# The first modulation's scale as two TensorE rows in place of eight columns

## The chip, the core and the metric

The kernel runs on one core of a Trainium2 chip. The metric is the device time in microseconds (us) of one execution. The engines are named as the profile names them: PE (TensorE, with its weight loads as PEld), DVE (VectorE), ACT (ScalarE), POOL (GpSimd) and SP (SyncE, which issues the DMAs).

## What is computed

A transformer block of 2048 tokens with 1024 channels, all in fp32. A vector `c` of 1024 numbers modulates it: six vectors of 1024 come out of one product with `w_mod` (1024 x 6144), two of which, the shift `sa` and the scale `ca`, are needed before anything else.

```python
mod = (_silu(c) @ w_mod).reshape(c.shape[0], 6, 1, -1)
sa, ca, ga, sb, cb, gb = (mod[:, 0], mod[:, 1], mod[:, 2], mod[:, 3], mod[:, 4], mod[:, 5])
h = _layernorm(x, axis=-1) * (1 + ca) + sa
x = x + ga * _A_ref(h, A_wq, A_wk, A_wv, A_wo, A_beta)   # attention, 32 heads, 4 segments of 512 tokens
h = _layernorm(x, axis=-1) * (1 + cb) + sb
x = x + gb * _B_ref(h, B_w1, B_b1, B_w2, B_b2)           # MLP across the tokens
return x
```

The attention goes through four segments of 512 tokens; each segment's queries see their own segment by softmax and the earlier ones through a memory matrix.

## The kernel before

**The whole.** Products that must be nearly exact are made of three reduced products (`float32r`): each operand is split into a high part (a cast, L123 on ACT or L125 on DVE) and a low part (the difference, L126 on DVE or POOL). The order of the instructions on each engine comes from the tile framework's scheduler at build time, so it is fixed when the kernel runs: each engine takes its queue in order and waits on semaphores. The change lies in the first part, up to the projection of the first segment; the rest of the program (attention L322 to L650, the mixer from L814) is untouched.

**The first part, in the order of the code.**

- `sc` (L110) is silu of `c`, laid out as 128 partitions x 8; `scb` (L257 to L263) is the same vector as a row that stands on all 128 partitions, made by eight transposes into the banks `scps` and two copies.
- `load_x` (L210) fetches four x tiles of 128 tokens, x0 to x3, for segment 0; `norm_x` (L215) normalizes each: statistics on DVE (L131 to L139), the affine step on ACT (L218).
- The modulation loop (L278) goes over eight chunks `ct` of 128 channels. For each it fetches two tiles of `w_mod`, 512 KB each, in buffers `wm` (11 of them): part 0 for the shift, part 1 for the scale. The shift is one DVE instruction that multiplies the tile by `scb` and sums each row into `saca[:, ct, 0]` (L283). The scale is made in two ways: for the first four chunks (`NSC = 4`) by eight PE products with a 128x128 piece of the tile as the stationary operand and one column of `sc` moving (L291); for the last four by two POOL products with `scb` (L287) and a sum on ACT (L288). L295 adds 1 and puts it in `saca[:, ct, 1]`.
- Within the loop the first three rounds also fetch and split the projection's first weights (`load_part`, L164: `wv`, `wq`).
- `h_chunk` (L220) transposes one chunk of channels of the four x tiles (L223, into a bank `hps`), applies scale and shift on ACT while it reads the bank (L225), and splits the result: the cast on ACT, the difference on POOL in segment 0; in segment 1 the cast on DVE, the difference on POOL for even chunks and on DVE for odd ones.
- `first_chunk` (L267) adds one chunk to the projections of segment 0: 12 products for keys and values (L196, banks `nps`) and 3 for queries (L204, bank `qps`).

**What comes next.** `project(0, ...)` (L338) copies `nps` out on ACT (L358, L359, L364), transposes the keys (L373, bank `kps`), splits queries and keys into `sg` and makes phi of the keys (L391 and L392 on ACT, L394 on DVE). `seg_load(1)` (L560) fetches x4 to x7, behind the last modulation tile, and normalizes them; `seg_chunks(1, 0, 8)` makes segment 1's eight h chunks; `project(1, ...)` uses them. SP issues all these DMAs from one queue, in its program order; a DMA also waits for the eighth one before it.

## Time and profile before

| what | value |
|---|---|
| runs | 2251.84, 2254.03, 2257.36 us; median 2254.03 |
| profiled execution | 2248.92 us, of which the span is 2247.2 us |
| granted clock, mean | 0.998 |
| PE / DVE / ACT / POOL busy | 98% / 74% / 51% / 33% of the span |
| DMA | 423.06 MB, mean 188 GB/s |

How to read it. The page gives busy times over the span. A line of a timeline is: start in us from the span's start, duration in us (from the first start to the last end, where several like instructions are merged), engine, line of the code, operation, output tile <- input tiles, shape, count, and in brackets the idle time of the engine ahead of it and what ended it. Matmuls are pipelined: a record lasts longer than the distance to the next start, so a merged row holds one such tail. A plain fp32 matmul is recorded as two instructions, a `float32r` one and a transpose as one. A line of the windows gives, for one stretch, the busy time and count of PE, PEld, DVE, ACT and POOL, the granted clock, the DMA engines' busy share, and GB/s.

### The profile page before, as it was taken

What the parts mean: (1) busy time and instruction counts of PE and PEld (TensorE: products, weight loads), DVE (VectorE), ACT (ScalarE), POOL (GpSimd) and SP (SyncE); (2) the same over time, 40 slices, a digit from 0 to 9 for tenths busy, and PEclk for the clock granted to TensorE, in tenths of its full rate; (3) what the DMA queues carried; (4) which work ended last, traced back from release to release, by engine and by line L of the source; (5) the groups of instructions that cost most, each with busy time, mean ns of one, the idle gap of its engine ahead of it and who ended that gap; (6) DMA issues with size and microseconds to landing.
All of it is one profiled execution on the core that took longest, in us unless ns stands there. A gap on an engine that the chain in (4) does not pass through costs nothing.

```text
span 2247.2 us, 38365 instructions
## 1 busy us (share of the span) xinstructions
PE 2195.4 (98%) x13802; PEld 1892.9 (84%) x13802; DVE 1671.5 (74%) x3778; ACT 1145.6 (51%) x2106; POOL 748.6 (33%) x847
## 2 busy tenths in 40 slices
PE   7999999999999999999999999999999999999999
PEld 6879888888988888988888888888888888888887
DVE  6676777766767777655758866788888887868687
ACT  6476867765666656655546633533334242424232
POOL 5166657656666667654001200033330000000000
PEclk9999999999999999999999999999999999999999
DMA  6656565687666566664764587755556541414134
GB/s 263 204 169 174 160 185 161 199 283 239 176 182 207 168 188 193 190 198 164 229 220 151 215 333 262 262 190 221 206 202 238 203 154 57 155 57 146 57 122 150
DMA packets 175186, 423.06 MB, mean 188 GB/s; under 512 B 17524, under 2 KB 71828, under 8 KB 166036
## 3 DMA queue, kind: packets, MB, share of 16 engines
q1 hardware_dynamic: 174996, 420.61, 57.1%
q8 instruction: 110, 1.80, 0.3%
q14 instruction: 80, 0.66, 0.1%
HBM read 244.62 MB, written 125.06 MB: 165 GB/s over the span
## 4 chain that ended last, share of the span: by engine, by line
PE 83%; DVE 7%; DMA 3%; POOL 2%; ACT 2%; issue 2%; SPq 1%; ACTq 0%; DVEq 0%; POOLq 0%
PE mx L863 44%; PE nps L196 11%; PE po L733 8%; PE qps L204 7%; PE pv L505 3%; PE a L476 1%; PE sx L441 1%; PE sz L441 1%; POOL ph L491 1%; DMA wr<-in_w_dram 1%; DVE ac L870 1%; PE a L479 1%; PE rd L413 1%; PE a L483 1%; PE sy L441 1%
## 5 line engine op out<-in xcount | busy, mean ns | idle before, releaser
L863 PE MATMUL mx<-bU,sp 128*128 128x512 f32 x2352 | 534.7, 389 | 1.1 <-DVE ac L870 0.9
L863 PEld LDWEIGHTS mx<-bU,sp 128*128 128x128 f32 x2352 | 441.0, 188 | 94.3 <-issue 1.3
L196 PE MATMUL nps<-wv,h 128*128 128x256 f32 x3072 | 441.7, 284 | 4.7 <-POOL h L126 3.8
L123 ACT CAST sp<-wr 128x384 fp32r<-128x384 f32 (+2 forms) x408 | 217.1, 545 | 430.5 <-PE mx L863 349.6
L491 POOL TENSOR_TENSOR ph<-p,ph 128x640 f16<-128x640 f32 x256 | 378.5, 1499 | 170.2 <-ACT ph L489 169.6
L863 PE MATMUL mx<-bA,sp 128*128 128x512 f32 x1764 | 430.5, 389 | 0.0
L196 PEld LDWEIGHTS nps<-wv,h 128*128 128x128 f32 x3072 | 405.6, 190 | 13.1 <-POOL h L126 5.0
L863 PEld LDWEIGHTS mx<-bA,sp 128*128 128x128 f32 x1764 | 331.1, 188 | 68.8
L126 DVE TENSOR_TENSOR sp<-wr,sp 128x384 fp32r<-128x384 f32 (+2 forms) x408 | 260.1, 648 | 31.5 <-ACT sp L123 31.3
L870 DVE TENSOR_TENSOR ac<-mx,ac 128x512 f32<-128x512 f32 x280 | 189.9, 686 | 85.2 <-PE mx L863 84.8
L204 PE MATMUL qps<-h,wq 128*128 128x512 f32 x768 | 196.3, 397 | 0.0
L489 ACT CAST ph<-p 128x1280 f16<-128x1280 f32 x128 | 160.9, 1257 | 51.6 <-POOL p L487 50.9
L733 PE MATMUL po<-wo,ots 128*128 128x512 f32 x768 | 181.3, 391 | 0.0
L487 POOL TENSOR_SCALAR_AFFINE_SELECT p<-p 128x256 f32<-128x256 f32 x256 | 131.7, 524 | 108.4 <-ACT p L484 54.8
L733 PEld LDWEIGHTS po<-wo,ots 128*128 128x128 f32 x768 | 142.7, 188 | 29.1
L863 PE MATMUL mx<-bB,sp 128*128 128x512 f32 x588 | 164.0, 389 | 0.0
L204 PEld LDWEIGHTS qps<-h,wq 128*128 128x128 f32 x768 | 140.9, 189 | 26.8 <-ACT vp L364 0.3
L442 DVE CUSTOM_DVE_ANT_0 sx<-sx,mask 128x128 f32<-128x128 f32 (+1 forms) x256 | 110.6, 432 | 65.4 <-PE sx L441 63.6
L505 PE MATMUL pv<-vp,ph 128*128 128x97 bf16 (+1 forms) x2560 | 141.9, 202 | 5.2 <-DVE red L512 2.8
L505 PEld LDWEIGHTS <-ph 128*128 128x128 f16 x2560 | 113.6, 98 | 28.7 <-issue 11.9
L863 PEld LDWEIGHTS mx<-bB,sp 128*128 128x128 f32 x588 | 110.4, 188 | 22.9
L870 DVE TENSOR_TENSOR cc<-mx,cc 128x512 f32<-128x512 f32 x140 | 95.0, 685 | 38.3 <-PE mx L863 38.1
(200 smaller groups left out, 3191.7 us busy)
## 6 DMA issues: line engine op xcount, KB each, us to landing
sk<-sg SPq DMA_DIRECT2D x384, 128.0 KB
wr<-in_w_dram SPq DMA_DIRECT2D x28, 1024.0 KB
wr<-in_w_dram SPq DMA_DIRECT2D x32, 768.0 KB
bstu<-ucd SPq DMA_DIRECT2D x28, 768.0 KB
wsp<-wv SPq DMA_DIRECT2D x32, 512.0 KB
rawm<-in_wm_b_dram SPq DMA_DIRECT2D x32, 512.0 KB
wv<-wsp SPq DMA_DIRECT2D x32, 512.0 KB
pcd<-cc SPq DMA_DIRECT2D x14, 1024.0 KB
```

Of the source, the lines that this page charges most:

```text
L123: last_hi[0] = A.copy(hi, src)
L126: lo_eng.tensor_tensor(lo, src, hi.bitcast(F32), op=ALU.subtract)
L196: T.matmul(ps[:, aa], h[:, j, 128 * tt:128 * tt + 128], wt[:, i, o:o + 256], start=(n == 0), stop=(n >= 6 * NK - 2), skip_group_check=True)
L204: T.matmul(ps, wt[:, i, o:o + 128], h[:, j], start=(k + n == 0), stop=(3 * k + n == 3 * NK - 1))
L442: marks[4 * t + h - LEADS, "V"] = V.tensor_tensor_reduce(o, o, mask[:, 384 - 128 * i:], 1.0, -3.0e38, op0=ALU.add, op1=ALU.max, accum_out= ...
L487: G.affine_select(w, w, pattern=[[0, 2], [1, 128]], compare_op=ALU.is_ge, fill=0.0, base=0, channel_multiplier=-1)
L489: marks[n, "A"] = A.copy(ph[:, 0], p32)
L491: marks[n, "G"] = G.tensor_tensor(ph[:, 1, c], p32[:, c], ph[:, 0, c], op=ALU.subtract)
L505: T.matmul(pv[:, i, 0:w], ph[:, part, o:o + 128], d["vp"][:, j, h, 0:w], start=(n == 0), stop=(n == 19), skip_group_check=True)
L733: T.matmul(ps, os_[:, i, P * ct:P * ct + P], wop[ct, nh][:, j], start=(n == 0), stop=(n == 3 * NK - 1))
L863: T.matmul(ps, ops[q][:, i, P * k:P * k + P], b[:, j], start=(m == 0 and first), stop=(m == 3 * nk - 1), skip_group_check=True)
L870: V.tensor_tensor(d, ps, d, op=ALU.add)
```

## The change

The scale is no longer made chunk by chunk. The host lays its half of `w_mod` out anew, as eight tiles of 512 KB: tile `i` holds, for one half of the output channels (512 columns), two blocks of 128 inputs. PE makes each half as one row of 512: the stationary operand is one column of `sc` (128x1), the moving one the 128x512 block of `w_mod`, eight such plain fp32 matmuls add up in one bank (`srow`). DVE copies the row from PSUM into partition 0 of `bc`, PE turns each 128 of it into a column by a product with the 1x1 corner of the identity (four products a half, into the bank `scale`), and one DVE instruction a half adds 1 and writes four columns of `saca`. The POOL products, the ACT sums and `scs` are gone.

The eight scale tiles are fetched ahead: four before x0 to x3, four after them, all before the first shift tile. The shift is made as before.

```diff
@@ -253,6 +252,15 @@
+    scale_wm = []
+
+    def fetch_scale(i):
+        t = s1p.tile([P, 2, 512], F32, tag="wm", bufs=11, name=f"wms{i}")
+        SY.dma_start(t.rearrange("p a n -> p (a n)"), wm_a[1, i])
+        scale_wm.append(t)
+
+    for i in range(4):
+        fetch_scale(i)
     xs = {0: [load_x(s1p, tt) for tt in range(4)]}
@@ -273,26 +281,25 @@
     with tc.high_priority():
         for t in xs[0]:
             norm_x(s1p, t)
-    scale_ps = bank("ms", 1, "scale")
-    scs = s1p.tile([P, NK], F32, name="scs")
+    for i in range(4, 8):
+        fetch_scale(i)
+    scale_ps = bank("pv", 1, "scale")
+    rows = bc.rearrange("p a b -> p (a b)")[0:1]
+    for cb in range(2):
+        ps = bank(*(("ms", 1), ("s1", 2))[cb], f"srow{cb}")
+        for k in range(NK):
+            T.matmul(ps[0:1], sc[:, k:k + 1], scale_wm[4 * cb + k // 2][:, k % 2], start=(k == 0), stop=(k == NK - 1))
+        V.tensor_copy(rows[:, 512 * cb:512 * cb + 512], ps[0:1])
+        for ct in range(4 * cb, 4 * cb + 4):
+            T.matmul(scale_ps[:, ct:ct + 1], rows[:, P * ct:P * ct + P], ident[0:1, 0:1], start=True, stop=True,
+                     skip_group_check=True)
+        V.tensor_scalar_add(saca[:, 4 * cb:4 * cb + 4, 1], scale_ps[:, 4 * cb:4 * cb + 4], 1.0)
     for ct in range(NK):
-        for part in range(2):
-            wm = s1p.tile([P, D], F32, tag="wm", bufs=11, name=f"wm{ct}_{part}")
-            last_wm = SY.dma_start(wm, wm_a[part, ct])
-            if part == 0:
-                V.scalar_tensor_tensor(wm, wm, 1.0, scb, op0=ALU.mult, op1=ALU.mult, accum_out=saca[:, ct, 0:1])
-            elif ct >= NSC:
-                for i in range(2):
-                    c = slice(512 * i, 512 * i + 512)
-                    G.tensor_tensor(wm[:, c], wm[:, c], scb[:, c], op=ALU.mult)
-                A.activation(wm, wm, AF.Copy, accum_out=scs[:, ct:ct + 1])
-            else:
-                for k in range(NK):
-                    T.matmul(scale_ps[:, ct:ct + 1], wm[:, P * k:P * k + P], sc[:, k:k + 1], start=(k == 0),
-                             stop=(k == NK - 1), skip_group_check=True)
+        wm = s1p.tile([P, D], F32, tag="wm", bufs=11, name=f"wm{ct}")
+        last_wm = SY.dma_start(wm, wm_a[0, ct])
+        V.scalar_tensor_tensor(wm, wm, 1.0, scb, op0=ALU.mult, op1=ALU.mult, accum_out=saca[:, ct, 0:1])
         if ct < 3:
             load_part(0, 0, *(("v", 0), ("q", 0), ("v", 1))[ct], W[0, 0])
-        V.tensor_scalar_add(saca[:, ct, 1:2], (scale_ps if ct < NSC else scs)[:, ct:ct + 1], 1.0)
         h_chunk(s1p, xs[0], 0, ct)
         if ct:
             first_chunk(ct - 1)
@@ -1065,9 +1072,8 @@
-        "wm_a": np.stack([wm[:, :D].T.reshape(NK, P, D), np.concatenate([
-            wm[:, D:2 * D].reshape(NK, P, NK, P).transpose(2, 1, 0, 3).reshape(NK, P, D)[:NSC],
-            wm[:, D:2 * D].T.reshape(NK, P, D)[NSC:]])]),
+        "wm_a": np.stack([wm[:, :D].T.reshape(NK, P, D),
+                          wm[:, D:2 * D].reshape(4, 2, P, 2, 512).transpose(3, 0, 2, 1, 4).reshape(NK, P, D)]),
```

1 line of the change is left out of this document (removed).

## The prediction

> **What bounds the kernel now.** I read the page first, then busy time in windows of 10 us, then the timeline of the first 70 us, where the change lies.
>
> ```profile
> span 2247.2 us, 38365 instructions
> PE 2195.4 (98%) x13802; PEld 1892.9 (84%) x13802; DVE 1671.5 (74%) x3778; ACT 1145.6 (51%) x2106; POOL 748.6 (33%) x847
> ```
> ```profile
> 10.00:20.00 10.00, 7.81 (x36) 7.44 (x37) 8.40 (x30) 7.81 (x13) 0.00 (x0) 1.00 1.03 411
> ...
> 40.00:50.00 10.00, 7.20 (x51) 6.25 (x50) 6.66 (x25) 6.95 (x17) 9.01 (x8) 1.00 0.01 4
> 50.00:60.00 10.00, 7.55 (x48) 6.14 (x48) 4.96 (x12) 10.00 (x19) 5.68 (x14) 0.87 0.13 28
> 60.00:70.00 10.00, 9.38 (x76) 8.98 (x76) 9.16 (x13) 4.20 (x6) 4.46 (x5) 0.96 0.95 263
> 70.00:80.00 10.00, 9.98 (x68) 8.87 (x67) 4.22 (x11) 4.71 (x11) 0.00 (x0) 1.00 0.95 341
> ```
> PE is busy for 98% of the span, but not at its start. A window's columns are PE, PEld, DVE, ACT, POOL, granted clock, DMA share, GB/s. From 70 us on PE works 9.98 us of 10. Before that others lead: the transfers at 10 to 20 (share 1.03), POOL at 40 to 50 (9.01), ACT at 50 to 60 (10.00).
>
> ```profile
> 31.42 5.01 POOL L287 TENSOR_TENSOR wm<-wm,scb 128x512 f32<-128x512 f32 x4
> 38.61 3.52 POOL L287 TENSOR_TENSOR wm<-wm,scb 128x512 f32<-128x512 f32 x2
> 43.32 2.53 POOL L287 TENSOR_TENSOR wm<-wm,scb 128x512 f32<-128x512 f32 x2
> 49.33 1.29 POOL L126 TENSOR_TENSOR h<-h,h 128x512 fp32r<-128x512 f32 x1 [0.99 <-DVE mv L133]
> 49.34 1.11 PE L196 MATMUL nps<-wv,h 128*128 128x256 f32 x8
> 51.46 1.11 PE L196 MATMUL nps<-wv,h 128*128 128x256 f32 x8
> 52.40 0.63 PE L204 MATMUL qps<-h,wq 128*128 128x512 f32 x2
> 57.75 1.49 ACT L225 ACTIVATE h<-hps,saca 128x512 f32<-128x512 f32 x2
> 68.94 5.73 PE L196 MATMUL nps<-wv,h 128*128 128x256 f32 x48 [0.53 <-POOL h L126]
> ```
> There are three stages. Stage 1 ends at 53.0 (52.40 + 0.63) with the eighth chunk of segment 0's projection; POOL holds it, with the scale's products (5.0 + 3.5 + 2.5 = 11.1 us) ahead of its h subtractions, the last of which ends at 50.6. Stage 2 runs to 68.94: x4 to x7 are normalized and become segment 1's h chunks, of which the first reaches ACT at 57.75. Stage 3 begins at 68.94, and PE is saturated from there. So the end moves by what 68.94 moves, and no more.
>
> **The change part by part.** Removed are the 11.1 us on POOL, four ACT sums and PE's 64 one-column products. Added on PE are 16 matmuls in plain fp32, one stationary column and 512 moving ones each (two instructions a matmul, as L291 and L423 have), and eight small products; on DVE two copies of a row and two adds in place of eight. The x tiles now land after four scale tiles, the shift tiles after all eight.
>
> ```profile
> 12.19 3.57 PE L291 MATMUL scale<-sc,wm 128*128 128x1 f32 x16 [3.42 <-DMA wm<-in_wm_a_dram]
> 17.17 3.41 PE L291 MATMUL scale<-sc,wm 128*128 128x1 f32 x16
> 21.91 3.57 PE L291 MATMUL scale<-sc,wm 128*128 128x1 f32 x16 [0.80 <-DVE saca L295]
> 26.94 1.20 PE L196 MATMUL nps<-wv,h 128*128 128x256 f32 x4
> 32.61 1.84 PE L291 MATMUL scale<-sc,wm 128*128 128x1 f32 x16
> 63.20 1.06 PE L423 MATMUL up<-v,pk 128*128 128x132 f32 x8
> 31.92 0.85 PE L204 MATMUL qps<-h,wq 128*128 128x512 f32 x3
> 59.38 1.20 PE L196 MATMUL nps<-wv,h 128*128 128x256 f32 x4
> ```
> ```profile
> 58.00:60.00 2.00, 1.45 (x8) 1.38 (x8) 1.76 (x4) 2.00 (x4) 0.89 (x1) 0.50 0.61 127
> ```
> *The clock.* The same 16 instructions take 3.57 us at 12 and at 22 us, and 1.84 at 32.6: PE runs at half rate until about 30 us. The granted column shows 1.00 there for want of a record; where it shows 0.50 (58 to 60), L196 takes 0.30 us apiece (59.38; 26.94 is the same), against 0.14 at 49.34.
>
> *The price of a 512-column fp32 instruction* is not in the trace. The lower bound is L204's single-pass rate: (0.85 - 0.39 for the tail) / 2 = 0.23 us. The upper bound is L423, the same kind of operands with 132 columns: (1.06 - 0.28) / 7 = 0.111 us, and 0.111 x 512 / 132 = 0.43. I take 0.43, the row of the same kind; doubled at half clock. A scale tile (two matmuls, four instructions) is then 1.72 us, 3.45 at half clock. [...]
>
> ```profile
> 6.83 1.94 PE L262 MATMUL scps<-ident,bc 128*128 128x128 f32 x8 [6.83 <-DVE bc L258]
> 40.22 1.03 PE L223 MATMUL hps<-ident,x 128*128 128x128 f32 x8
> 15.25 1.22 DVE L283 SCALAR_TENSOR_TENSOR wm<-wm,scb 128x1024 f32<-128x1024 f32 x1
> 19.35 1.29 DVE L126 TENSOR_TENSOR wq<-rawq,wq 128x512 fp32r<-128x512 f32 x2 [0.88 <-ACT wq L123]
> 21.95 0.78 ACT L225 ACTIVATE h<-hps,saca 128x512 f32<-128x512 f32 x1 [0.24 <-DVE saca L295]
> 28.93 0.62 ACT L123 CAST h<-h 128x512 fp32r<-128x512 f32 x1
> 36.91 1.74 POOL L126 TENSOR_TENSOR h<-h,h 128x512 fp32r<-128x512 f32 x1 [0.48 <-ACT h L123]
> ```
> ```profile
> L870 DVE TENSOR_TENSOR ac<-mx,ac 128x512 f32<-128x512 f32 x280 | 189.9, 686 | 85.2 <-PE mx L863 84.8
> ```
> *Stage 1 anew.* At 411 GB/s a 512 KB transfer takes 1.28 us; the sixth released L291 at 12.19, so the first lands at 5.8 and the k-th 1.28 (k - 1) later: scale tiles at 5.8 to 9.6, x0 to x3 by 14.7, the other scale tiles at 16.0 to 19.8, the shift tiles from 21.1 (in the new order of DMAs the 13th) to 35.1 (the 24th, as before). PE's queue in the changed program stands thus: tile 0, the eight scb transposes, tiles 1 to 3, four small products, tiles 4 and 5, and tiles 6 and 7 with x transposes between. Tile 0 at half clock: 5.8 + 3.45 = 9.3. I let the clock be free from there, since PE then streams without a pause. Transposes (1.0) 10.3; three tiles 15.5, and 16.0 for a late window. Now a wait is added: PE's small products stand behind DVE's copy of the row (between nothing and 0.69, L870 with as many elements a partition; I take 0.69), and DVE's copy stands behind PE, ahead of x3's statistics. Copy to 16.9 with its hand-over, eight instructions at L291's full-clock 0.115: 17.9. Four tiles and four x transposes (6.9 + 0.5): 25.3. The second copy and products and the rest of the transposes bring PE to chunk 0 at 27.3. DVE, which waited at 25.3 for the row, has wv's low half, a shift sum and wq's low half to do (0.7 + 1.29 + 1.22 + 0.65) until 29.4, so chunk 0 ends at 29.6, and chunk 1, after its h (0.78 + 0.62) and POOL (1.3 to 1.74), at 33.0. After that PE alone sets the pace: six chunks at 2.12 (49.34 to 51.46) and four sets of transposes at 0.5 make 14.7: **stage 1 ends at 47.7**, 5.3 us earlier. The shift is not late: DVE comes to its last sum at about 38.6, and h7 is complete by 41.5, ahead of chunk 7 at 45.6. The SP queue's new waits for PE (shift tiles 3 to 7 take the buffers of scale tiles 0 to 4) are over by 20 us, and the DMAs concerned stand to be issued from 18 to 25; nothing is held.
>
> ```profile
> 50.78 2.36 ACT L218 ACTIVATE x<-x,mv 128x1024 f32<-128x1024 f32 x2
> 53.05 0.35 ACT L358 COPY k<-nps 128x256 f32<-128x256 f32 x1
> 54.62 1.27 ACT L218 ACTIVATE x<-x,mv 128x1024 f32<-128x1024 f32 x1
> 55.76 0.60 ACT L123 CAST sg<-qps 128x512 fp32r<-128x512 f32 x1
> 59.08 0.67 ACT L392 ACTIVATE rk<-rk 128x512 f32<-128x512 f32 x1
> 61.32 0.69 DVE L394 SCALAR_TENSOR_TENSOR pk<-k,rk 128x512 f32<-128x512 f32 x1
> ```
> *Stage 2 gives it back.* In before, ACT normalizes x4 to x6 while PE finishes stage 1, and only x7 follows (54.62). In the changed program's order all four stand behind the copies out of nps, so behind stage 1's end. ACT's queue from nps on: six copies 1.6 (53.05 to 54.62), x4 to x6 at 1.18 (3.5), the four small operations 2.0 (55.76 to 57.75), rk 0.6, then DVE's pk 0.7, which is now ahead of x7's scalars, x7 1.1, and 1.2 for the scalars between and the transposes: 10.7, from 0.7 before stage 1's end. The first h chunk of segment 1 comes 10.0 after the end, where it was 4.75 (57.75 - 53.0): 57.7, as good as unchanged. What is left is that rk and pk no longer stand in the stretch from there to stage 3: about 0.6. Sum: 5.3 - 5.25 + 0.6 = **0.7 us earlier**. The profiled execution took 2248.92 (1.7 us lie around its span), so 2248.2; the median of the runs is 5.1 above it, and I apply the sum to the median: 2253.3.
>
> **The rivals.**
>
> *The clock stays at half rate through the scale rows.* From 17 to 25 us PE was full of one-column products and transposes, and the clock did not come free (21.91: 3.57); it came free at about 30, after 3 us of L196 and L204 from 26.94 on. If what counts is how much of the array works, one stationary column is next to nothing. Then tile 0 ends at 9.3, transposes (1.94) 11.2, three tiles 21.5, copy and products at half rate 24.2, four tiles and transposes 39.0, chunk 0 from 42.8 to 46.9, seven more 64.2: 16.5 later than forecast, and stage 2 follows it, 15.8 slower than before: 2269.8. Each 2 us that the clock stays at half beyond 9.3 cost 1; the forecast's 0.7 is gone after 1.4 us, and 0.3% is lost if the clock is still at half at about 24 (9.3 + 2 x 7.5). For it speaks the row at 21.91; against it that those products stream a single column in 0.22 us, while the new ones stream without a gap.
> [...]
>
> *The fp32 instruction costs the lower bound, 0.23.* Then transfers and DVE set stage 1: the first row at 14.0, the second at 20.7, x3's transposes at 22, chunk 0 done at 26.9, chunk 1 at 30.0, the end at 44.7. Three us more: 2250.3. Against it: L423's spacing, though 132 columns may hide behind their weight load there.
>
> *Stage 2 follows stage 1 down*, if the copies and normalizations overlap better than their queue says: all 5.3 and 0.6 kept, 2248.1. Against it is ACT at 10.00 of 10 in that window.
>
> **How the numbers follow.** Chances: the forecast 0.53 (its own range 2250.5 to 2256: a clock 3.4 us late, 1.7, the hand-overs not priced, runs that lie 2.2 below and 3.3 above their median); half clock 0.24; the lower price 0.17; stage 2 following 0.06. To leave out no more than 2 in 10 the range must take in the half clock: 2247 to 2270. About 0.3% (6.8 us) is what a measurement of this kernel can tell from no change: faster than that is only the last rival with luck, 0.07; slower is the half clock, 0.24; within, 0.69.
>
> **What would show it.** In the changed profile: L291's 32 instructions with the row's tile, 0.43 us from start to start at full rate, 0.86 at half; the end of the second row at about 25; POOL with no work on wm; the eighth chunk's end near 47.7; x4's normalization on ACT after the copies of k and v; segment 1's first h at about 57.7; the run of nps products on which stage 3 starts at about 68. Wrong would be the forecast if the second row ends after 33 (the clock) or before 22 (the price), or if x4 is normalized before stage 1 ends.

## The result, and the profile after

The changed kernel takes **2270.27 us** (median of 6 runs, 2265.20 to 2274.89) against 2254.77 for the kernel before on the same chip (6 runs, 2250.21 to 2258.01): a ratio of 1.0071, 95% interval 1.0052 to 1.009, or 15.5 us slower. The forecast was 2253.3 with a range of 2247 to 2270, so the result lies just above the range. The profiled execution took 2268.45 us.

First the head of the page of the changed kernel, then its busy time in windows (columns: length, PE, PEld, DVE, ACT, POOL, granted clock, DMA share, GB/s).

```profile
span 2266.7 us, 38307 instructions
PE 2207.5 (97%) x13786; PEld 1891.1 (83%) x13786; DVE 1669.2 (74%) x3774; ACT 1143.6 (50%) x2098; POOL 746.2 (33%) x839
```
```profile
20.00:30.00 10.00, 9.49 (x39) 3.59 (x36) 5.61 (x14) 8.01 (x13) 1.41 (x1) 1.00 1.03 410
30.00:40.00 10.00, 0.00 (x0) 0.00 (x0) 10.00 (x18) 3.50 (x6) 10.00 (x1) 0.62 0.96 383
40.00:50.00 10.00, 9.84 (x54) 9.16 (x55) 1.54 (x4) 2.79 (x4) 4.83 (x5) 0.70 0.01 2
...
90.00:100.00 10.00, 10.00 (x51) 8.62 (x50) 6.50 (x17) 4.81 (x10) 0.00 (x0) 0.83 0.88 324
```

The page's sums hide what happened: POOL has even less work than before. The second window shows it. From 30 to 40 us PE does nothing at all, DVE is busy for all 10 us, and POOL is "busy" for 10 us with one instruction (x1). The timeline of that stretch, and the same instruction among POOL's groups (count, then busy us and mean ns):

```profile
5.88 3.57 PE L291 MATMUL srow<-wms,sc 128*1 128x512 f32 x4 [5.88 <-DVE sc L110]
11.28 5.16 PE L291 MATMUL srow<-wms,sc 128*1 128x512 f32 x11
...
18.62 3.60 PE L291 MATMUL srow<-wms,sc 128*1 128x512 f32 x8
26.61 0.68 DVE L292 COPY bc<-srow 1x512 f32<-1x512 f32 x1 [1.45 <-PE srow L291]
27.21 1.27 DVE L125 TENSOR_TENSOR wv<-rawv,wv 128x512 fp32r<-128x512 f32 x2
28.41 1.21 DVE L300 SCALAR_TENSOR_TENSOR wm<-wm,scb 128x1024 f32<-128x1024 f32 x1
28.59 11.51 POOL L125 TENSOR_TENSOR h<-h,h 128x512 fp32r<-128x512 f32 x1 [19.73 <-ACT h L122]
28.73 0.72 PE L195 MATMUL nps<-wv,h 128*128 128x256 f32 x4
29.56 0.07 DVE L300 DVE_READ_ACCUMULATOR wm<-wm,scb 128x1 f32 x1
29.63 1.27 DVE L125 TENSOR_TENSOR wq<-rawq,wq 128x512 fp32r<-128x512 f32 x2
30.83 1.21 DVE L300 SCALAR_TENSOR_TENSOR wm<-wm,scb 128x1024 f32<-128x1024 f32 x1
...
37.76 1.21 DVE L300 SCALAR_TENSOR_TENSOR wm<-wm,scb 128x1024 f32<-128x1024 f32 x1
38.91 1.27 DVE L130 BATCH_NORM_STATS2 st<-x 128x6 f32<-128x512 f32 x2
40.16 2.07 PE L195 MATMUL nps<-wv,h 128*128 128x256 f32 x8 [10.48 <-POOL h L125]
60.55 0.37 ACT L365 COPY k<-nps 128x256 f32<-128x256 f32 x1 [0.59 <-PE nps L195]
60.82 0.63 PE L203 MATMUL qps<-h,wq 128*128 128x512 f32 x2
62.23 1.29 ACT L217 ACTIVATE x<-x,mv 128x1024 f32<-128x1024 f32 x1
71.80 2.12 ACT L224 ACTIVATE h<-hps,saca 128x512 f32<-128x512 f32 x3 [0.85 <-PE hps L222]
82.20 4.36 PE L195 MATMUL nps<-wv,h 128*128 128x256 f32 x36 [0.35 <-POOL h L125]
88.86 0.44 PE L380 MATMUL kps<-ident,k 128*128 128x128 f32 x2 [1.34 <-ACT k L365]
```
```profile
L125 POOL TENSOR_TENSOR h<-h,h 128x512 fp32r<-128x512 f32 x12 | 26.1, 2183 | 33.4 <-ACT h L122 28.6 <-DVE h L124 4.7
```
```profile
L126 POOL TENSOR_TENSOR h<-h,h 128x512 fp32r<-128x512 f32 x12 | 16.9, 1414 | 27.9 <-ACT h L123 18.3 <-DVE h L125 8.6 <-DVE mv L133 1.0
```

The second of these two groups is the kernel before: the same 12 subtractions, 9.2 us less in all (26.1 - 16.9), and one instruction makes up that difference: the other eleven of after take 14.6 together. POOL's low half of h_0 starts at 28.59 and ends at 40.10, 11.51 us where before has 1.26 to 1.83 for the same form. PE waits 10.48 for it. Meanwhile DVE runs through wv's low half, the remaining shift sums and wq's low half with no gap: the sums (1.21 us each) and the half tiles (some 0.64) with two operands in SBUF. When the last shift sum ends (37.76 + 1.21 = 38.97) and single-operand statistics follow, POOL's instruction ends 1.13 later.

### The profile page after: what moved, and what is told of

The parts are those of the page before. It is cut to its first block, busy times and chain, and to the rows that moved or that the text cites. A ratio compares the mean times of both kernels' runs of the same rounds, so it can differ in the third digit from the quotient of the medians.

```text
span 2266.7 us, 38307 instructions
## 1 busy us (share of the span) xinstructions
PE 2207.5 (97%) x13786; PEld 1891.1 (83%) x13786; DVE 1669.2 (74%) x3774; ACT 1143.6 (50%) x2098; POOL 746.2 (33%) x839
## 4 chain that ended last, share of the span: by engine, by line
PE 84%; DVE 4%; DMA 4%; ACT 2%; POOL 2%; issue 2%; SPq 1%; ACTq 0%; DVEq 0%; POOLq 0%
PE mx L870 47%; PE nps L195 11%; PE qps L203 7%; PE po L740 6%; PE pv L512 3%; PE sx L448 1%; PE a L483 1%; PE sz L448 1%; POOL ph L498 1%; PE a L486 1%; PE srow L291 1%; DMA rawm<-in_wm_b_dram 1%; DMA sk<-sg 1%; PE rd L420 1%; PE a L490 1%
## 5 line engine op out<-in xcount | busy, mean ns | idle before, releaser
L195 PEld LDWEIGHTS nps<-wv,h 128*128 128x128 f32 x3072 | 408.2, 191 | 19.5 <-POOL h L125 11.3
L125 DVE TENSOR_TENSOR sp<-wr,sp 128x384 fp32r<-128x384 f32 (+2 forms) x408 | 259.6, 647 | 25.3 <-ACT sp L122 25.1
```

The source lines that it names most:

```text
L125: lo_eng.tensor_tensor(lo, src, hi.bitcast(F32), op=ALU.subtract)
L195: T.matmul(ps[:, aa], h[:, j, 128 * tt:128 * tt + 128], wt[:, i, o:o + 256], start=(n == 0), stop=(n >= 6 * NK - 2), skip_group_check=True)
```

## The experiments

Times of the first stage in each kernel, from the timelines (us): the first low half of h_0 on POOL, the first copy of k (the end of stage 1, less half a microsecond to one, except in before, old_scale_first, lo_dve_x47, lo_dve_norm, x47_first and the three x_between kernels, where ACT does other work ahead of it), the first h chunk of segment 1, and the result. The diffs below show the lines that decide, not every line.

| kernel | first low half on POOL | first k | first h of segment 1 | median (runs) | ratio to before |
|---|---|---|---|---|---|
| before | 2.95 for the first two | 53.05 | 57.75 | 2254.8 (6) | 1 |
| after | 11.51 | 60.55 | 71.80 | 2270.3 (6) | 1.0071 |
| lo_on_dve | on DVE | 48.50 | 59.19 | 2260.6 (11) | 1.0027 |
| shift_waits | 13.99 for the first three | 60.24 | 71.48 | 2272.2 (5) | 1.0079 |
| shift_stats | 1.29 | 47.28 | 58.44 | 2254.5 (10) | 1.0008 |
| lo_dve_x47 | on DVE | 54.15 | 58.37 | 2253.1 (11) | 1.0003 |
| x47_first | 11.50 | 62.41 | 69.16 | 2270.8 (5) | 1.0082 |
| shift_gaps | 3.45 | 51.43 | 62.89 | 2260.3 (5) | 1.0033 |
| x_between | 3.44 | 54.76 | 49.36 | 2249.8 (11) | 0.998 |
| lo_dve_norm | on DVE | 52.89 | 54.99 | 2252.8 (12) | 0.9994 |
| old_scale_first | 2.25 | 54.95 | 60.18 | 2260.5 (11) | 1.0019 |
| x_between_dve | on DVE | 56.09 | 53.83 | 2253.9 (12) | 0.9993 |
| row_on_act | 1.29 | 48.64 | 59.88 | 2257.7 (12) | 1.0014 |
| x_between_act | 1.29 | 54.10 | 48.70 | 2249.0 (12) | 0.9979 |
| row_wide | 2.31 | 50.76 | 61.99 | 2263.0 (8) | 1.004 |

After, shift_waits, shift_stats, x47_first and row_on_act have one and the same order of instructions in the later stages. In the others the scheduler ordered the later groups anew, which moves single groups by several microseconds back and forth (in lo_on_dve the later copies of k come between 4.3 us earlier and 16.6 later than in before); of those, the first 70 us are evidence and the total only in part.

### Is it DVE's unbroken run that holds POOL?

**lo_on_dve**: segment 0's low halves go to DVE.
```diff
-        split(pg, h32, V if seg else A, V if seg and ct % 2 else G)
+        split(pg, h32, V if seg else A, G if seg and ct % 2 == 0 else V)
```


> Theory A (VectorE's unbroken run of two-source instructions keeps GpSimd from reading its operands): with segment 0's eight low halves on VectorE, GpSimd has nothing to wait for. The first low half ends near 31.5 us instead of 40.1, the others follow VectorE's queue (a shift sum of 1.21 and a low half of 0.67 each), the eighth by 47 to 49, the last chunk by 50 to 52 instead of 61, TensorE's gap of 10.5 us is gone, and the time is 9 to 13 us below after's: 2256 to 2261. Theory B (the rows themselves, the clock or the order of the loads cost the time): TensorE stays idle until about 40 whichever engine subtracts, and the time stays within 3 us of after's, 2267 to 2273.

Measured: ratio 1.0027 (1.0015 to 1.004). Stage 1 ends 12 us earlier than in after (48.50 against 60.55) and the total falls by about 10. Most of the loss goes when POOL isn't asked. That does not yet say what it collides with.

**shift_waits**: each shift sum is told to be issued after the low half two chunks earlier.
```diff
+            if ct > 1:
+                s.enter_context(tc.issue_after(lows[0, ct - 2].ins))
```


> The low halves stay on GpSimd; VectorE's shift sum of column ct is queued behind the low half of column ct-2, so that VectorE's queue has gaps. Theory A: the first low half ends by 34 instead of 40.1, each further round costs a shift sum and a low half one after the other (1.21 + 1.28 and the hand-overs, 2.7 to 3.0), the eighth ends by 53 to 55, the last chunk by 57: 3 to 7 us below after, 2263 to 2267. Theory B, or VectorE's work in itself: more waits on VectorE only add to it, the time is 2270 or above.

Measured: ratio 1.0079 (1.0066 to 1.0091). The order to issue did not become a wait between the engines: the built program has the instructions of after, one for one. It is a repeat of after, and the long subtraction is there again: the first three take 13.99 us, as in after. As a test of the wait it says nothing.

**shift_stats**: each shift sum is replaced by two single-operand statistics of the same tile. It leaves out the shift.
```diff
-        V.scalar_tensor_tensor(wm, wm, 1.0, scb, op0=ALU.mult, op1=ALU.mult, accum_out=saca[:, ct, 0:1])
+        for i in range(2):
+            V.bn_stats(s6[:, i], wm[:, 512 * i:512 * i + 512])
+        V.tensor_scalar(saca[:, ct, 0:1], s6[:, 0, 1:2], 0.0, None, op0=ALU.mult)
```


> The eight shift sums are left out: in the place of each, VectorE takes two statistics of the same tile, which read one source, for about the same time (1.2 to 1.3 us), and writes the shift as zero. Theory A in its narrow form (two-source reads alone shut GpSimd out): the first low half ends by 34, while VectorE is still busy without a gap until 39 or so; the last chunk by 52, the time 8 to 13 us below after. Theory A in its wide form (any unbroken run of VectorE shuts GpSimd out) and theory C (GpSimd waits for VectorE's queue by a dependency): the first low half still ends near 40, right after the run, and the time is that of after within 3 us.

Measured: ratio 1.0008 (0.9994 to 1.0023), 15.8 us below after, more than the 8 to 13 expected. The timeline of POOL and the window from 30 to 40 in shift_stats:
```profile
27.91 1.29 POOL L125 TENSOR_TENSOR h<-h,h 128x512 fp32r<-128x512 f32 x1 [19.04 <-ACT h L122]
```
```profile
30.00:40.00 10.00, 9.97 (x74) 9.02 (x74) 10.00 (x23) 8.37 (x13) 6.46 (x5) 1.00 0.97 385
```
DVE is busy for all 10 us here too, and yet POOL's subtraction takes 1.29 and PE works 9.97 of 10. So it is not how much DVE has to do, but what: POOL is held by the shift sums, which have two operands in SBUF, and not by the statistics, which have one, 11.51 against 1.29. What the two engines share there is not shown. Nor is it shown why POOL had to wait so long: up to the next boundary between DVE's instructions it would have been one sum, 1.21 us, and here it lost every boundary for 10 us. That is the open part, taken up below.

### Is the rest of the loss in stage 2's order on ACT?

**lo_dve_x47**: lo_on_dve, and the copies of k and v issued behind x6's normalization, as in before.
```diff
+    with tc.issue_after(normed[2].ins):
+        project(0, 0)
+        project(0, 1)
```


> As lo_on_dve, and besides the k and v copies of segment 0 stand behind the normalization of x6 in ScalarE's queue, so that x4 to x6 are normalized before the last chunk ends. Theory D (segment 1's start hangs on ScalarE's order, as the prediction's step on stage 2 had it): the first h of segment 1 comes 3 to 6 us earlier than in lo_on_dve and the time is 2 to 5 us below it, 2251 to 2257. Rival E (other work, the raw weights of the next group and the stack copies, is late by then anyway): the first h moves and the time does not, within 1 us of lo_on_dve.

Measured: 1.0003 (0.9994 to 1.0012), 7.5 us below lo_on_dve; but the first h of segment 1 came only 0.8 earlier (58.37 against 59.19). The gain isn't made in stage 2, and can't be put down to this edit, since the later order is another one.

**x47_first**: that order of ACT alone, in after.
```diff
-    project(0, 0)
-    project(0, 1)
     with tc.issue_after(last_wm.ins):
         seg_load(1)
+    with tc.issue_after(normed[2].ins):
+        project(0, 0)
+        project(0, 1)
```


> After's kernel, with the low halves on GpSimd, and only ScalarE's order changed: the k and v copies of segment 0 stand behind the normalization of x6. Theory A: the collision is untouched, the first low half still ends near 40 and the last chunk near 61. Theory D (stage 2 has a share of its own, by ScalarE's order): the first h of segment 1 comes 4 to 6 us earlier than after's 71.8 and the time is 3 to 7 us below after's, 2263 to 2267. Rival E: the time stays within 2 us of after's.

Measured: 1.0082 (1.0068 to 1.0096). The first h came 2.6 earlier (69.16 against 71.80), of which 1.4 was there already when POOL's first low half began (27.20 against 28.59); the copies of k came 1.9 later, and the total is after's. ACT's order in stage 2 does not hold the 15 us.

**lo_dve_norm**: lo_dve_x47 with x5 and x7 normalized on DVE.
```diff
+        if eng is V:
+            return V.tensor_scalar(t, t, mv[:, 2:3], mv[:, 3:4], op0=ALU.mult, op1=ALU.add)
```


> As lo_dve_x47, and VectorE normalizes x5 and x7 in the place of ScalarE, which is busy for 9.9 of the 10 us from 50 to 60 in that kernel. Theory D: the first h of segment 1 comes 2 to 4 us earlier than 58.4, the time 1 to 4 us below lo_dve_x47's, 2249 to 2252. Rival E: it moves the first h and not the time, 2253 within 1 us.

Measured: 0.9994 (0.9984 to 1.0004). The first h came at 54.99, 3.4 earlier than in lo_dve_x47, and the total moved by 0.3. Here too, a few microseconds of the first h in stage 2 did not arrive at the end.

**shift_gaps**: a real wait this time. POOL writes a zero made from its low half into the place that a later shift sum fills.
```diff
+        if seg == 0 and ct < NK - 2:
+            G.tensor_scalar(saca[:, ct + 2, 0:1], pg[:, 1, 0:1].bitcast(F32), 0.0, None, op0=ALU.mult)
```


> After's kernel, and GpSimd writes, after each low half of column ct, a zero made from that half to where VectorE puts the shift sum of column ct+2; so that sum really waits for the low half, which issue order alone did not bring about in shift_waits. Theory A: VectorE falls idle at about 30.5 behind the wq splits, the first low half ends at 31.8 to 32.5 instead of 40.1, a column then takes 2.6 to 2.9 us (a shift sum and a low half, one after the other), the eighth low half ends by 50 to 53, the k copy starts at 53 to 56, and the time is 4 to 9 us below after's, 2260 to 2265, though VectorE has more waits and GpSimd more work. Theories B and C: the added waits can only make it longer, 2270 or more.

Measured: 1.0033 (1.0021 to 1.0045). The timeline of shift_gaps:
```profile
29.14 1.27 DVE L125 TENSOR_TENSOR wq<-rawq,wq 128x512 fp32r<-128x512 f32 x2
31.90 2.29 DVE L302 SCALAR_TENSOR_TENSOR wm<-wm,scb 128x1024 f32<-128x1024 f32 x1 [1.49 <-POOL saca L229]
```
```profile
28.10 3.45 POOL L125 TENSOR_TENSOR h<-h,h 128x512 fp32r<-128x512 f32 x1 [19.79 <-ACT h L122]
```
DVE's run now breaks off at 30.41, and POOL's subtraction ends 1.14 later, at 31.55, about its own length. It stood there from 28.10 on and missed the boundaries in between. So the run as a whole holds it.

**x_between** and **x_between_dve**: x4 to x7 are loaded and normalized between the chunks of segment 0, with the low halves on POOL or on DVE.
```diff
+        if ct in (1, 2, 3, 4):
+            x47.append(load_x(s2p, 4 + len(x47)))
+            norm_x(s2p, x47[-1])
```


> After's kernel, with the loads of x4 to x7 set between those of the second to sixth shift tiles, so that VectorE's statistics of x4 to x7, which read one source, stand between the two-source shift sums; low halves on GpSimd. Theory A in its narrow form: GpSimd gets in at the first statistics, the first low half ends by 32 to 33.5, the last chunk by 54; x4 to x7 are normalized before that, and the first h of segment 1 comes by 48 to 54. If segment 1's start sets the end (theory D), 2244 to 2251, below both kernels. Rival E (raw weights and stack copies come no earlier): 2251 to 2255. Wide form of A: GpSimd stays shut out until about 40, 2262 or more.

> x_between with segment 0's eight low halves on VectorE, and x4 to x7 between the fourth to seventh shift tiles. If VectorE's queue has room for both (a shift sum of 1.21, a low half of 0.67 and two statistics of 0.6 for each column at 2.1 to 2.6 us of TensorE), the last chunk ends by 50 and the first h of segment 1 comes by 52: 2246 to 2250, at or a little below x_between's 2249.8. If VectorE becomes the bound, the low halves run late and it is 2251 to 2256.

Measured: 0.998 (0.9971 to 0.9989) and 0.9993 (0.9983 to 1.0003). In x_between the statistics of x4 break DVE's run at 30.07, so POOL's subtraction takes 3.44; the first h of segment 1 comes at 49.36, ahead of the copies of k. It is 0.2% faster than before, and 20 us faster than after. With the low halves on DVE (and the x tiles two chunks later, `ct in (3, 4, 5, 6)`) the gain is gone: DVE is then busy for 19.8 of the 20 us from 30 to 50, where it has 17.6 in x_between, and the first h comes at 53.83.

### Is it the order of the loads?

**old_scale_first**: the code of before, with the eight scale tiles loaded ahead of the shift tiles.
```diff
+        t = s1p.tile([P, D], F32, tag="wm", bufs=11, name=f"wm{ct}_1")
+        SY.dma_start(t, wm_a[1, ct])
```


> The kernel before, with its old way to the scale (no rows: four column blocks by one-column products on TensorE, four by GpSimd and ScalarE); only its loads are put in after's order, all eight scale tiles ahead of the eight shift tiles. Theory A': not the rows but the order of the loads makes the collision, since VectorE then has nothing but two-source work for some 10 us, one tile after another: GpSimd's first low half of segment 0 takes 6 us or more and ends with VectorE's run, at 36 to 41; the last chunk ends by 57 to 62, and the time is 2262 to 2272. Rival F (the rows are needed for it, by the copy that keeps VectorE's work back until 26): low halves of 1.3 to 2.3 us as in the kernel before, the first by 34, the last chunk by 54, the time 2249 to 2258. The later stages may be issued in another order, so the first 65 us tell more than the total.

Measured: 1.0019 (1.001 to 1.0027). The low halves are those of rival F; the time, 2260.5 with another order of the later stages, is above its 2249 to 2258. The timeline of old_scale_first:
```profile
36.37 2.31 DVE L291 SCALAR_TENSOR_TENSOR wm<-wm,scb 128x1024 f32<-128x1024 f32 x1
```
```profile
38.07 1.75 POOL L126 TENSOR_TENSOR h<-h,h 128x512 fp32r<-128x512 f32 x1 [0.47 <-ACT h L123]
```
The same late, dense shift sums meet the same subtractions, and the two engines take turns: DVE's sum takes 2.31 with its wait for POOL, POOL's subtraction 1.75. A dense run of DVE is not enough. Something else in after makes POOL lose every boundary.

### What makes POOL lose its turns

**probe** and **probe_row** compute nothing of the reference: bursts of DVE instructions in a row, with a POOL subtraction of 128x512 that becomes ready within each.
```text
probe:      10 bursts of sums, subtractions and statistics in several mixtures
probe_row:   9 bursts in after's own order, with the column that L296 adds from
             PSUM or SBUF, POOL released by DVE or ACT, POOL used just before,
             loads under way, sums in place
```


> None of the reference is computed: ten short bursts on tiles of the two shapes, with 8 us or more between them, in which VectorE runs 10 to 12 instructions in a row and GpSimd's 128x512 subtractions are released in the middle of the row (bursts 0 to 4, 7, 8), or together with its first instruction (5 and 6), or GpSimd copies, reading one source (9). Theory A as far as it is shown (a first low half that comes into a row of two-source instructions waits until the row ends): bursts 0 to 3: GpSimd's first instruction ends 1.2 us after the row's last one, so some 9 to 10 us long in burst 0 and 6 in burst 2; burst 4: it gets in at the first statistics, 2 us later; burst 9: the copy is not held. Theory G (GpSimd gets in at every boundary between two of VectorE's instructions, as in old_scale_first): no GpSimd instruction takes over 2.5 us and every VectorE instruction that follows one is lengthened by some 1.1 us. Bursts 5 and 6 tell whether a stream of GpSimd that begins with the row alternates with it, as in old_scale_first, even where a single late one is shut out: if so, A holds for an instruction that comes late and G for one that comes first.

> None of the reference is computed: nine bursts of VectorE in after's own order (two splits, a shift sum, the column of 1 + scale from PSUM, two splits, a shift sum, two splits, four shift sums, some 12 us in all), with one 128x512 subtraction of GpSimd released by ScalarE in the first shift sum, as h_0's low half is. probe showed that GpSimd gets in at the next boundary in plain rows, so what shuts it out in after is something that probe did not have. One burst each leaves out or changes one thing: 1 without the column from PSUM, 3 released by VectorE, 4 the column from SBUF, 5 GpSimd busy shortly before, 6 and 7 with loads of 512 KB running, with and without the column, 8 the shift sums in place. Theory H (the short column instruction between a shift sum and a split makes GpSimd lose its turn, and it does not ask again until VectorE pauses): 8 us or more in bursts 0, 2, 3, 5, 6, 8, under 2.5 us in 1 and 7. Theory I (the running loads do it): 8 us or more in 6 and 7 alone. Theory J (the first subtraction of a program is long): burst 0 alone. If all nine take under 2.5 us, none of these is the cause.

Measured: no subtraction in either is long. In probe one takes 1.64 to 2.24 among two-operand instructions, and three in a row take 6.52:
```profile
18.16 2.18 POOL L56 TENSOR_TENSOR pl<-a,dv 128x512 fp32r<-128x512 f32 x1 [17.72 <-DVE dv L32]
42.65 6.52 POOL L56 TENSOR_TENSOR pl<-a,dv 128x512 fp32r<-128x512 f32 x3 [22.30 <-DVE dv L32]
```
All the theories tested there fell: the unbroken run by itself, and in probe_row the column's source, the engine that releases POOL and the loads (its last burst, with sums in place, broke apart on its loads). One thing that after's run had and these hadn't was its first instruction, the copy of the scale's row, **1x512**.

**row_on_act**: the two copies of a row go to ACT; nothing else is changed.
```diff
-        V.tensor_copy(rows[:, 512 * cb:512 * cb + 512], ps[0:1])
+        A.copy(rows[:, 512 * cb:512 * cb + 512], ps[0:1])
```


> After's kernel; the two copies of the scale rows from PSUM, one partition wide, are made by ScalarE in the place of VectorE; every later instruction stays in after's order. Theory K (the one-partition copy at the head of VectorE's unbroken run is what makes GpSimd lose its turns): the first low half takes 2.5 us or less and ends by 32, VectorE and GpSimd alternate as in old_scale_first (shift sums of 2.2 to 2.3 us), the eighth low half ends by 50, the last chunk by 54, and the time is 8 to 14 us below after's: 2254 to 2262. Theory A in its first form (any unbroken two-source run shuts GpSimd out): the first low half still ends at 39 to 40.5 and the time is after's within 2 us.

Measured: 1.0014 (1.0003 to 1.0026), 12.5 us below after with the same order of everything else. The timeline of row_on_act, and its window:
```profile
27.30 1.29 POOL L125 TENSOR_TENSOR h<-h,h 128x512 fp32r<-128x512 f32 x1 [18.27 <-ACT h L122]
29.67 2.34 POOL L125 TENSOR_TENSOR h<-h,h 128x512 fp32r<-128x512 f32 x1 [1.08 <-ACT h L122]
32.48 1.82 POOL L125 TENSOR_TENSOR h<-h,h 128x512 fp32r<-128x512 f32 x1 [0.47 <-ACT h L122]
48.91 0.63 PE L203 MATMUL qps<-h,wq 128*128 128x512 f32 x2
```
```profile
33.08 2.31 DVE L300 SCALAR_TENSOR_TENSOR wm<-wm,scb 128x1024 f32<-128x1024 f32 x1
```
```profile
30.00:40.00 10.00, 8.83 (x62) 7.29 (x61) 10.00 (x13) 6.03 (x10) 6.81 (x4) 1.00 0.98 390
```
The first low half begins while DVE is idle (DVE's run starts at 27.77), so the test is the later ones: POOL and DVE take turns again (2.34 and 2.31), PE works 8.83 of the 10 us, and stage 1 ends at 49.54. With an instruction of 0.68 us moved off DVE, whose result only chunks 4 to 7 use, POOL is no longer kept waiting for 10 us.

**probe_one** and **probe_phase**: bursts in after's order, each headed by a copy of another width or source; probe_phase has three heads (one partition from PSUM, one from SBUF, 128 partitions from SBUF), each with five moments at which POOL becomes ready. Neither computes anything of the reference.
```diff
+        copy(0, q, n, q if sbuf else ps)
         for i, f in enumerate([tt, tt, stt, tt, tt, stt, tt, tt, stt, stt, stt, stt, bn]):
+                    G.tensor_tensor(pg[:, 1], h32, pg[:, 0].bitcast(F32), op=ALU.subtract)
```


> None of the reference is computed: ten bursts like those of probe_row (twelve two-source instructions of VectorE, one subtraction of GpSimd released in the first shift sum), headed by one instruction of VectorE, with no gap behind it: in 0 and 9 a statistics instruction on all partitions, in 1 and 2 a 1x512 copy from PSUM, in 3 the same from SBUF, in 4 a 128x512, in 5 a 32x512, in 6 a 64x512 copy from PSUM; in 7 one single-source instruction stands behind the first shift sum, in 8 two statistics stand between the 1x512 copy and the row. Theory K: 8 us or more in 1, 2 and 3, under 2.5 us in 0, 4 and 9; 5 and 6 tell whether less than the whole width is enough; 7 about 2.5 to 4 us; 8 tells whether the state outlives other instructions. If all ten are under 2.5 us, the copy's width is not the cause.

> None of the reference is computed: fifteen bursts of the row of probe_one, in five groups of three; the heads of a group are a 1x512 copy from PSUM, a 1x512 copy within SBUF and a 128x512 copy within SBUF, and from group to group GpSimd's request comes some 0.07 to 0.1 us earlier, by a narrower copy of ScalarE ahead of it. Theory K1 (the kind of head decides): all five SBUF one-partition bursts take 8 us or more, all five PSUM ones and all five controls under 2.5 us. Theory K2 (behind a one-partition head the turn is a matter of the moment of the request): long and short ones among both kinds of one-partition heads, none among the controls. Theory K3 (the copy within SBUF decides, whatever its width): the controls are long too.

Measured in probe_one: 10.21 us behind a copy of 1x512 within SBUF, and 2.06 to 2.16 behind every other head: 1x512 from PSUM, 32, 64 and 128 partitions, statistics. In probe_phase one line of each head, with the copy ahead of it and an accumulator's read behind:
```profile
14.68 0.68 DVE L41 COPY one<-ps 1x512 f32<-1x512 f32 x1 [14.68 <-ACT ps L73]
16.69 2.16 POOL L82 TENSOR_TENSOR pg<-h,pg 128x512 fp32r<-128x512 f32 x1 [16.25 <-ACT pg L81]
29.85 0.41 DVE L41 COPY one<-q 1x512 f32<-1x512 f32 x1 [2.33 <-ACT q L72]
31.67 10.20 POOL L82 TENSOR_TENSOR pg<-h,pg 128x512 fp32r<-128x512 f32 x1 [12.82 <-ACT pg L81]
32.54 0.07 DVE L41 DVE_READ_ACCUMULATOR dv<-q,b 128x1 f32 x1
50.68 0.43 DVE L41 COPY one<-q 128x512 f32<-128x512 f32 x1 [9.32 <-ACT q L72]
52.50 2.06 POOL L82 TENSOR_TENSOR pg<-h,pg 128x512 fp32r<-128x512 f32 x1 [10.63 <-ACT pg L81]
53.37 0.09 DVE L41 DVE_READ_ACCUMULATOR dv<-q,b 128x1 f32 x1
```
The one-partition copy within SBUF shuts POOL out in 5 of 5 (10.20 to 10.42, until the row ends), whenever POOL becomes ready; the same copy over 128 partitions in 0 of 5 (2.06 to 2.28); the one-partition copy from PSUM, which is after's, in 0 of 5 (2.15 to 2.31). Over this range the moment is not what decides.

**probe_all**: 12 bursts with after's head from PSUM, each with a circumstance of after (PE making the row, PE and ACT busy, loads, sums in place and others), two of them with the head within SBUF.
```diff
+            for k in range(8):
+                T.matmul(row[0:1], q[:, k:k + 1], b[:, 0:512], start=(k == 0), stop=(k == 7))
-        copy(0, q, n, q if sbuf else ps)
+        copy(0, q, 1, q if sbuf else row)
```


> None of the reference is computed: twelve bursts of the row of probe_one. The head is a 1x512 copy from PSUM in 0 to 9, within SBUF in 10 and 11. Burst 0 is plain; 1 adds running loads, 2 a stream of ScalarE copies, 3 TensorE (the row made by one-column products, and products running beside), 4 sums in place, 5 a two-source sum shortly before the head, 6 splits whose halves share a tile, as the weights' do, 7 TensorE and ScalarE, 8 these and loads, 9 all of them and the column from PSUM. If a circumstance makes the copy from PSUM act as one within SBUF does, its burst and 9 are 8 us or more and 0 is 2.2; if 9 alone is long, it takes several; if all of 0 to 9 are under 2.5 us, what makes the difference stays open, and only the one-line change of row_on_act shows that the copy matters in the changed kernel. Bursts 10 and 11 are long if the rule for copies within SBUF holds under load and behind another sum.

Measured: behind the head from PSUM the subtraction is long in 2 of 10 bursts, the one whose row PE had made, and the one with PE, ACT and loads together; but in two others that also had PE make the row it takes 1.84 and 1.91. Both heads within SBUF are long (10.21). The long and a short one of those with PE:
```profile
98.35 10.21 POOL L119 TENSOR_TENSOR pg<-h,pg 128x512 fp32r<-128x512 f32 x1 [23.89 <-ACT pg L118]
195.09 1.84 POOL L119 TENSOR_TENSOR pg<-h,pg 128x512 fp32r<-128x512 f32 x1 [23.26 <-ACT pg L118]
```
So a one-partition head from PSUM can do what after shows. Both long bursts are among the four whose row PE had made, and of the 13 others behind a one-partition head from PSUM (with those of probe_one and probe_phase) none is long; what decides among the four stays open.

**row_wide**: the row is made on all 128 partitions (the stationary operand is the broadcast column), and DVE copies 128x512 in the same place of its queue. The rows have a tile of their own, and the tiles of wm ten buffers in place of eleven.
```diff
-            T.matmul(ps[0:1], sc[:, k:k + 1], scale_wm[4 * cb + k // 2][:, k % 2], start=(k == 0), stop=(k == NK - 1))
-        V.tensor_copy(rows[:, 512 * cb:512 * cb + 512], ps[0:1])
+            T.matmul(ps, bc[:, k], scale_wm[4 * cb + k // 2][:, k % 2], start=(k == 0), stop=(k == NK - 1))
+        V.tensor_copy(rows[:, 512 * cb:512 * cb + 512], ps)
```


> After's kernel; the stationary operand of the scale rows is the column of sc repeated 128 times, so that each row stands on all 128 partitions, and VectorE copies 128x512 in the place of 1x512, at the same place of its queue; the buffers of the modulation tiles are 10 in the place of 11, for room. The first part's order is after's on every engine that matters, the later order is another one. Theory K (the width of the copy): VectorE's row has the longer hand-overs (the accumulator's read 75 to 85 ns, not 70), GpSimd's first low half takes 2.5 us or less and ends by 32, the last chunk ends at 47 to 51, and the time is 2252 to 2262. If the width does not matter, the first low half ends at 38 to 41 and the time is 2266 or more.

Measured: 1.004 (1.0026 to 1.0054), just above what was expected, with another order of the later stages. The timeline of row_wide:
```profile
26.70 0.69 DVE L292 COPY rows<-srow 128x512 f32<-128x512 f32 x1 [1.20 <-PE srow L291]
28.53 2.31 POOL L125 TENSOR_TENSOR h<-h,h 128x512 fp32r<-128x512 f32 x1 [19.66 <-ACT h L122]
29.72 2.27 DVE L125 TENSOR_TENSOR wq<-rawq,wq 128x512 fp32r<-128x512 f32 x2
```
The copy comes at the same time (26.70 against 26.61), from PSUM, just as long, in the same place, and POOL is let in at the first boundary: 2.31 in place of 11.51. With row_on_act this puts the cause, within the kernel, on the copy's **single partition**, at the head of a run of DVE without a gap. What else row_wide changes (PE's wider stationary operand, the tile of the rows, the ten buffers) is not separated there; in probe_phase, between the copies within SBUF, the width alone differs.

**x_between_act**: x_between with the rows copied on ACT.
```diff
-        V.tensor_copy(rows[:, 512 * cb:512 * cb + 512], ps[0:1])
+        A.copy(rows[:, 512 * cb:512 * cb + 512], ps[0:1])
```


> x_between with the two row copies on ScalarE, all else in x_between's order. Its first low half ended at 31.3 and the second at 33.6, some 3 us after row_on_act's; if the early low halves set the end, the last chunk ends 1 to 3 us earlier and the time is 1 to 3 us below 2249.8; if the loads of the last shift tiles or VectorE's queue set it, the time is within 1 us of x_between's.

Measured: 2249.04 (12 runs), ratio 0.9979 (0.9967 to 0.9991). It is within 1 us of x_between, as expected if not the early low halves but the loads or DVE's queue set the end. The two are the only kernels here that are faster than before clear of the noise.

## Why the prediction was wrong

**The price of the fp32 instruction was right.** Eight of them take 3.60 from 18.62, which is 0.43 from start to start and the last one's tail (0.59 in all); at half clock four take 3.57 from 5.88, 0.86 apart with a tail of 1.0. Rival 2 with 0.23 is refuted.

**The clock was right in kind, and its moment varies.** In after's trace it came free at about 11.9, not 9.3: eleven instructions take 5.16 us from 11.28, where 4.9 would be the full rate (10 x 0.43 + 0.59), so no more than the first half microsecond of them is at half. That is 6 us after the rows began at 5.88, with 2 us of transposes among them. In row_on_act, whose PE has the same instructions up to there, it came free after 2.6 us:
```profile
6.05 3.17 PE L291 MATMUL srow<-wms,sc 128*1 128x512 f32 x4 [6.05 <-DVE sc L110]
9.15 1.09 PE L270 MATMUL scps<-ident,bc 128*128 128x128 f32 x8
```
Four instructions in 3.17 are three at 0.86 and one at the full rate, and the transposes take 1.09 where after has 1.97. Only rows of one stationary column had run by then, so a stream through one such column did free the clock here. Rival 1 is refuted; that its time (2269.8) lies within a microsecond of the result is a coincidence, since the scale rows run at the full rate and the loss has another origin. The two traces have 6.0 and 2.6 us, so this case gives no single figure. The forecast's half microsecond "for a late window" and the 3.4 us by which its own range lets the clock be late are terms that no run shows; against the forecast's 9.3 the clock came free at 11.9 in after, 2.6 later, and at 8.6 in row_on_act (6.05 + 3 x 0.86), 0.7 earlier.

**The second row and chunk 0's start** came at 26.61 and 28.73, against 25.3 and 27.3: 1.4 late, most of it the clock (2.6 us more at half rate cost 1.3). In row_on_act chunk 0 begins at 27.34, as forecast.

**The step that failed is this: "so chunk 0 ends at 29.6, and chunk 1, after its h (0.78 + 0.62) and POOL (1.3 to 1.74), at 33.0. After that PE alone sets the pace".** The price of POOL's low half, 1.3 to 1.74, was taken from rows of before. For chunk 0 the forecast let only DVE's low half of wq set the end and gave POOL's low half of h_0 no term at all; it was just this one that took 11.51. Chunk 0 ended at 43.08 in place of 29.6, and PE, which "alone sets the pace", stood still for 10.48. Stage 1 ended at 61.45 (60.82 + 0.63) in place of 47.7, 13.75 later. Of that, 1.4 is the late start; 10.5 less the 1.5 of waiting that the forecast itself held is 9.0; and a third loss followed from the pause, the clock, which fell back to half while PE was idle: granted 0.62 of the window from 30 to 40 (0.50 from 36 to 46) and 0.70 of the one from 40 to 50, where it cost 3.0 us (row_on_act, without the pause, has 1.00 in both). Together 13.4 of 13.75. That POOL's instruction was held by DVE is shown (shift_stats, shift_gaps), and that the copy of one partition ahead of the run is what made POOL lose its turns is shown in the kernel from two sides (row_on_act, row_wide).

**Stage 2's term was right.** The first h of segment 1 came 10.35 after stage 1's end (71.80 - 61.45), forecast 10.0, and x4 was normalized (62.23) behind the copies of k and v, as the queue said. Rival 3 is refuted. In row_on_act, with the collision gone, the distance is 10.34 (59.88 - 49.54).

**Stage 3 passed the delay on, and added a little.** Its run of nps products starts at 82.20 against 68.94, 13.3 late. Behind it PE waits 1.34 for a copy of k (88.86), and the granted clock is 0.83 from 90 to 100, 1.7 us, where before has 1.00 in the same work. That makes about 16; the third projection's first copy of k is 15.4 late (103.19 against 87.74), and the medians differ by 15.5. The profiled execution, 19.5 longer in span, also has later windows at a low clock (granted 0.72 from 526 to 532 and 0.66 from 779 to 784, where before's has 1.00).

**What the forecast would have been worth without the collision** is seen in row_on_act: 2257.74, 2.1 us above its before, where the forecast had 0.7 below. The structure (stage 1 shorter by some 3.5, stage 2 giving it back) held. Even there PE did not set the pace alone: from the forecast start stage 1 ended at 49.54, 1.8 later than forecast, and PE waited 0.36, 0.61 and 0.48 for low halves on POOL; stage 3 began at 70.26, where about 68 was forecast. The rivals lacked the mechanism that decided: each looked at PE, its clock, its price, its order, and none at a subtraction on POOL whose price depended on what DVE ran beside it (2.31 in row_wide, 11.51 in after).

## What to carry to other kernels

A duration read from the trace of before holds only as long as the neighbour does the same (POOL's low half took 1.26 to 1.83 in before, 11.51 in after); where a change makes one engine's run denser, price the other engine's instructions anew, with the rest of the run and its own time as the upper bound (in after 10.38 and 1.13). Keep DVE's copies of a single partition away from the head of a gapless run of two-operand instructions while POOL is on the path: with the copy on ACT the first subtraction took 1.29 and the kernel 12.5 us less, with the copy over all partitions 2.31 and 7.3 us less (with another order of the later stages). In the profile, look for one instruction that is many times its form's mean, and at what its neighbour does in that time: sums and shares of busy time count it as work.

## What the runs showed of the hardware

- **The lockout.** Behind a one-partition DVE copy within SBUF, POOL lost every boundary until the run ended in 8 of 8 bursts (10.2 to 10.4 us); behind one from PSUM in 2 of 17 bursts with an unbroken run, and in all five kernels that had it on DVE ahead of two-operand instructions and the subtraction (11.5 in after and x47_first, 13.99 for the first three in shift_waits as in after; about 3.45 in shift_gaps and x_between, where the run breaks). Behind a copy over 128 partitions it never happened (0 of 5 within SBUF, 0 of 1 from PSUM, and row_wide). Copies over 32 and 64 partitions were run once each, from PSUM, where even a single partition is mostly harmless; they show little (2.10 and 2.09 in probe_one).
- **The accumulator's read.** In after's locked-out run it takes 70 to 71 ns (the 0.07 at 29.56). But that goes with the narrow head and not with the lockout: in probe_phase it takes 0.07 behind a one-partition copy where POOL was shut out (32.54) and also where it was let in (17.63 and 69.54), and 0.08 to 0.09 behind 128 partitions (0.09 at 53.37). The shorter read is therefore not enough to shut POOL out.
- **Turns.** Without the lockout POOL comes in at the boundaries of DVE's run: a 128x512 subtraction of POOL goes from 1.28 to between 1.7 and 2.3 (1.82 and 2.34 in row_on_act, 1.72 to 2.31 in row_wide, 1.74 to 2.25 in old_scale_first), DVE's sum from 1.21 to 2.3 (2.31, 2.30, 2.31 there).
- **The clock.** A stream of 512 columns through one stationary column freed the clock 2.6 us (row_on_act) to 6.0 us (after) after it began; single-column products, filling 17.2 to 20.6 in before, did not free it: 16 of them take 3.57 at 21.91, as at 12.19, and 1.84 at 32.61.
